# Attention with all PSUM banks until the first layer begins, weight decoding moved, first batch's layer output kept in DRAM, branch at the end

## The chip, the cores and the metric

The kernel runs on one core of a Trainium2 chip. The metric is device microseconds of one execution. One profiled execution gives the trace; its rows are in us from the start of its span.

## The reference, cut to what matters

```
scores = q @ k.T / sqrt(64);  scores = cap * tanh(scores / cap)      # 4 batches, 12 heads, 448 tokens, head size 64, fp32
attn = exp(scores - max) / (sum + 1e-9);  x = attn @ v               # heads joined: x is 1792 x 768
h = max(x @ w1, x @ w2, x @ w3)                                      # layer 1, w 768 x 768
y = h @ moe_w_out                                                    # layer 2, 768 x 768
u = sigmoid(y @ w_gate) * (y @ w_val)                                # layer 3, 768 x 1536 each
out = u @ moe2_w_out                                                 # layer 4, 1536 x 768
```

q, k and v are float32, all seven weight matrices float64.

## The kernel before

**Numbers.** Weights arrive as pairs of 32-bit words. `widths` (L44) loads a block of 128x768 of them (768 KB, tile `wraw`) and decodes it into float32 (`wf`): one operation on ACT (L51), four on DVE (L52 to L55). `parts` (L58) splits `wf` into a rounded high part `wh` (ACT, L61) and the remainder `wl` (POOL, L62). `product` (L76) makes one 128x448 block of a layer for one batch: 18 matmuls, six each of high by high, high by low and low by high. `wraw`, `wf`, `wh` and `wl` have two buffers each, so weights run about two blocks ahead. `col_block` (L65) loads one such block; layer 1 needs 18 (six column blocks j of three matrices). For batch 0 they are decoded, and stored decoded in DRAM (`ws`); later batches load them from there.

**Attention.** Heads are taken in pairs: 24 pairs, six a batch. `prepare` (L108) turns a pair's k and q with TensorE into a PSUM tile `tr` and splits them into kh, kl, qh, ql. `Pair.scores` (L171) forms score groups 0, 1, 2 (896 columns, two PSUM banks) and a half group; ACT applies tanh (L190), which frees the PSUM, and exp (L198). Sums over the keys are formed by POOL (L201, group 0 + 1) and DVE (L203, L206). `weigh` (L208) multiplies by v, `finish` (L220) normalises on DVE and splits x (ACT L235, POOL L236). `sc` and `tr` share two buffers of two banks, `pv` has two banks, and the layer products the remaining two (`mm`).

**Order.** Iteration n of the loop at L427 emits: loads of pair n+2, scores of pair n, `weigh` and `finish` of pair n-1, `prepare(n+1)`; from n = 7 it also takes three steps of `first_layers` (L419), a step being one `product` of layer 1 for batches 0, 1 and 2. Batch 3's x goes to DRAM (`xs`, L238) and is read back after the attention (L457 to L462) for its layer 1, with all eight PSUM banks. Then layer 2 (six weight blocks, four batches), layer 3 (12 blocks j, each of gate and value weights for four batches) and layer 4. Layer 4 decodes the 12 blocks of `wo2` one by one (L354) while it accumulates its first four output tiles, and then does ten more tiles from the kept weights.

**Queues.** All loads and stores are issued on SP's queue, in order. The build moves instructions ahead of program order where buffers allow, so some matmuls of layer 1 stand between those of the attention; each engine then runs its list in order.

**Branch.** The whole computation stands twice: for a small cap (`compute(False)`, the path that runs) and for any cap (`compute(True)`). A flag made from cap is read by every engine at the start (L483), before the If.

## Time and profile before

| | |
|---|---|
| median of three runs (lowest, highest) | 1165.6 us (1165.25, 1174.87) |
| profiled execution: its time, its span | 1164.32 us, 1162.5 us |
| busy share PE, PEld, DVE, ACT, POOL | 96%, 80%, 44%, 39%, 28% |
| matmuls | 5640 |
| HBM read, written | 86.31 MB, 13.96 MB |

```
PE   5889889999999999999999999999999999899998
DVE  3765987734242424117333333333333336763331
ACT  3667557566665553333222111111111124443331
POOL 1323545454544444554110111111111112510000
```

Each digit is the busy share, in tenths, of one fortieth of the span (29 us). A busy PE is not a PE at its peak, since queued matmuls overlap: how many matmuls a stretch holds says more than its busy time.

### The profile page before, as it was taken

The page shows a single profiled execution, that of the slowest core. Times are in us where ns is not written, and L with a number is a line of the kernel's source. Part 1 is how long each engine was busy: PE and PEld are TensorE (multiplying, and loading weights), DVE is VectorE, ACT ScalarE, POOL GpSimd, SP SyncE. Part 2 cuts the span into 40 slices and gives each one's busy share as a digit, 9 for nine tenths or more (in the row PEclk, how much of TensorE's full clock was granted, in tenths as well). Part 3 has the DMA queues.
Part 4 walks back from the last instruction along what each step waited for, and adds up shares of the span by engine and source line. Part 5 has one row for each costly group of instructions (what it writes and reads, how often), then busy time and mean ns, then how long its engine had stood idle before and what let it go on. Part 6 is the DMA issues. An engine that isn't in the chain of part 4 may idle for free.

```text
span 1162.5 us, 14670 instructions
## 1 busy us (share of the span) xinstructions
PE 1110.2 (96%) x5640; PEld 932.2 (80%) x5640; DVE 508.1 (44%) x804; ACT 456.8 (39%) x754; POOL 328.0 (28%) x193
## 2 busy tenths in 40 slices
PE   5889889999999999999999999999999999899998
PEld 2335666677767677899999999999999999899997
DVE  3765987734242424117333333333333336763331
ACT  3667557566665553333222111111111124443331
POOL 1323545454544444554110111111111112510000
PEclk9999899999999999999999999999999999899999
DMA  4643465633333323333111111111111111420011
GB/s 102 184 130 91 127 179 167 206 103 101 93 101 102 86 84 103 114 109 119 55 55 55 55 55 55 55 55 55 55 55 55 55 55 55 162 68 31 28 36 36
DMA packets 123359, 101.32 MB, mean 87 GB/s; under 512 B 70544, under 2 KB 112528, under 8 KB 123280
## 3 DMA queue, kind: packets, MB, share of 16 engines
q1 hardware_dynamic: 123280, 100.29, 29.1%
q8 instruction: 46, 0.75, 0.3%
q14 instruction: 33, 0.27, 0.1%
HBM read 86.31 MB, written 13.96 MB: 86 GB/s over the span
## 4 chain that ended last, share of the span: by engine, by line
PE 55%; issue 2%; POOL 1%; DVE 1%; ACT 1%; DMA 0%; POOLq 0%
PE mm L80 43%; PE mm L323 12%; POOL w L359 1%; DVE wf L55 0%; DVE wf L54 0%; DMA xr<-xs 0%; ACT w L358 0%; ACT wf L51 0%; POOL w2last L359 0%; DVE us L318 0%; ACT x L461 0%; DVE o L338 0%; ACT us L317 0%; DVE wf L53 0%; DVE wf L52 0%
## 5 line engine op out<-in xcount | busy, mean ns | idle before, releaser
L62 POOL TENSOR_TENSOR wl<-wf,wh 128x768 fp32r<-128x768 f32 x102 | 193.4, 1897 | 481.0 <-PE mm L80 389.8
L80 PE MATMUL mm<-y,wh 128*128 128x448 f32 x1152 | 249.1, 365 | 0.0
L80 PEld LDWEIGHTS mm<-y,wh 128*128 128x128 f32 x1152 | 216.3, 188 | 17.1
L80 PE MATMUL mm<-x,wh 128*128 128x448 f32 x864 | 198.5, 375 | 5.5 <-ACT x L461 2.2
L80 PEld LDWEIGHTS mm<-x,wh 128*128 128x128 f32 x864 | 160.5, 190 | 36.4 <-issue 9.5
L61 ACT CAST wh<-wf 128x768 fp32r<-128x768 f32 x102 | 84.9, 832 | 158.0 <-PE mm L80 121.0
L323 PE MATMUL mm<-w,us 128*128 128x384 f32 x756 | 136.1, 339 | 5.8 <-POOL w L359 5.8
L323 PEld LDWEIGHTS mm<-w,us 128*128 128x128 f32 x756 | 133.8, 191 | 6.5 <-POOL w L359 6.4
L80 PE MATMUL mm<-y,wl 128*128 128x448 f32 x576 | 132.3, 365 | 0.0
L80 PEld LDWEIGHTS mm<-y,wl 128*128 128x128 f32 x576 | 108.2, 188 | 8.6
L80 PE MATMUL mm<-x,wl 128*128 128x448 f32 x432 | 100.1, 366 | 0.0
L292 DVE TENSOR_TENSOR u<-mm,sg 128x448 f32<-128x448 f32 x48 | 29.8, 621 | 158.8 <-PE mm L80 158.8
L190 ACT ACTIVATE e<-sc,tsc 128x896 f32<-128x896 f32 x96 | 84.4, 910 | 33.3 <-PE sc L185 33.1
L289 ACT ACTIVATE sg<-mm 128x448 f32<-128x448 f32 x48 | 26.2, 546 | 166.0 <-PE mm L80 166.0
L198 ACT ACTIVATE e<-e,capb 128x896 f32<-128x896 f32 x96 | 88.1, 951 | 0.9
L52 DVE TENSOR_SCALAR wf<-wf 128x768 f32<-128x768 f32 x60 | 41.4, 694 | 105.5 <-ACT wf L51 105.4
L80 PEld LDWEIGHTS mm<-x,wl 128*128 128x128 f32 x432 | 81.3, 188 | 6.9
L318 DVE TENSOR_TENSOR us<-u,us 128x128 fp32r<-128x128 f32 (+1 forms) x192 | 54.8, 304 | 71.9 <-ACT us L317 71.9
L51 ACT ACTIVATE wf<-wraw 128x768 f32<-128x768 f32 x60 | 54.6, 911 | 75.7 <-POOL wl L62 57.4
L54 DVE SCALAR_TENSOR_TENSOR wf<-wraw,wf 128x768 int32<-128x768 int32 x60 | 82.1, 1372 | 1.5
L203 DVE TENSOR_TENSOR sum<-sum,e 128x896 f32<-128x896 f32 x24 | 32.3, 1347 | 107.4 <-ACT e L198 91.2
L317 ACT CAST us<-u 128x128 fp32r<-128x128 f32 (+1 forms) x192 | 48.5, 284 | 77.0 <-PE mm L323 73.8
(83 smaller groups left out, 1200.9 us busy)
## 6 DMA issues: line engine op xcount, KB each, us to landing
wf<-ws SPq DMA_DIRECT2D x54, 384.0 KB, 3.1
wraw<-in_moe_w_dram SPq DMA_DIRECT2D x18, 768.0 KB, 4.7
wraw<-in_moe_w_out_dram SPq DMA_DIRECT2D x18, 768.0 KB, 4.3
wraw<-in_moe_w_gate_dram SPq DMA_DIRECT2D x12, 768.0 KB, 4.3
wraw<-in_moe_w_val_dram SPq DMA_DIRECT2D x12, 768.0 KB, 4.4
ws<-wf SPq DMA_DIRECT2D x18, 384.0 KB, 2.7
kn<-in_k_dram SPq DMA_DIRECT2D x24, 192.0 KB, 3.3
qn<-in_q_dram SPq DMA_DIRECT2D x24, 192.0 KB, 3.6
```

The source lines that it names most:

```text
L51: nc.scalar.activation(wf, high.bitcast(F32), AF.Abs)
L52: nc.vector.tensor_scalar(wf, wf, LEAST, MOST, ALU.max, ALU.min)
L54: nc.vector.scalar_tensor_tensor(wi, high, -0x40000000, wi, ALU.bitwise_and, ALU.bitwise_or)
L61: nc.scalar.copy(wh, wf)
L62: nc.gpsimd.tensor_sub(wl, wf, f(wh))
L80: nc.tensor.matmul(ps, a[:, c, :], x[:, m, c, :], start=(n == 0), stop=(n == len(passes) - 1))
L190: nc.scalar.activation(e, sc[:, :w, :S], AF.Tanh, scale=tsc)
L198: nc.scalar.activation(e, e, AF.Exp, scale=1.0 if self.general else capb)
L203: nc.vector.tensor_add(self.sum, self.sum, e)
L317: nc.scalar.copy(us[:, 0, t, d], s)
L318: nc.vector.tensor_sub(us[:, 1, t, d], s, f(us[:, 0, t, d]))
L323: nc.tensor.matmul(pss[hf][:, :HALF], us[:, a, t, :], w2[fc][ww][:, hf * HALF : (hf + 1) * HALF], start=(fc == 0 and m == 0), stop=(fc == ...
```

## The change

- The attention before layer 1 (n up to 6) has a PSUM pool of its own with three two-bank buffers for `sc` and `tr`; at n = 7 it is closed, and `mm` and the old pool of two buffers take its banks. Until n = 6, `prepare(n+1)` is emitted before `weigh` of pair n-1.
- After iterations 1 to 6, the first six weight blocks of layer 1 are decoded and stored in `ws`; batch 0 loads these and decodes the other twelve.
- For batch 0 of layer 1, the remainders `wl` and of h are formed on DVE; for pairs 4 to 12 the group sum and the remainder of x too (`adds`).
- Batch 3's x stays in SBUF, its layer 1 is part of the interleaved steps, and h of batch 0 (2.75 MB) goes to DRAM at n = 18 and comes back in six parts during the last steps. Layer 2 takes the batches in the order 1, 2, 3, 0. After the attention, six new banks and the two of `mm` are taken in turn.
- `wo2` is decoded in layer 3, a block per j, and stored in DRAM (`ws2`); layer 4 loads the decoded blocks.
- Loads of the first pair's q go on ACT's queue; the tail of q has a zero-filled tile of 128 rows; the first pair's kh and qh are copied by ACT.
- `compute(False)` always runs; the flag is read at n = 4 and the If around `compute(True)` stands at the end.

```diff
+    EARLY = 6
-    xs = dram.tile([KC, P, S], F32, name="xs")
+    hs = dram.tile([P, 2 * KC * S], F32, name="hs")
+    ws2 = dram.tile([NF, P, DM], F32, name="ws2")
...
-        nc.gpsimd.tensor_sub(wl, wf, f(wh))
+        (sub or nc.gpsimd.tensor_sub)(wl, wf, f(wh))
...
+        other = nc.scalar if n == 0 else nc.sync
-        nc.sync.dma_start(out=qn, in_=main(q))
+        other.dma_start(out=qn, in_=main(q))
...
-        copy = nc.vector.tensor_copy if n < NP else nc.scalar.copy
+        copy = nc.vector.tensor_copy if 0 < n < NP else nc.scalar.copy
...
+            self.adds = nc.vector if NP - 2 <= n <= 2 * NP else nc.gpsimd
...
-                nc.gpsimd.tensor_add(self.sum, self.e[0], self.e[1])
+                self.adds.tensor_add(self.sum, self.e[0], self.e[1])
...
-            if x is not None:
-                nc.scalar.copy(x[:, 0, p, :], xn)
-                nc.gpsimd.tensor_sub(x[:, 1, p, :], xn, f(x[:, 0, p, :]))
-            else:
-                nc.sync.dma_start(out=xs[p], in_=xn)
+            nc.scalar.copy(x[:, 0, p, :], xn)
+            self.adds.tensor_sub(x[:, 1, p, :], xn, f(x[:, 0, p, :]))
...
+                sub = None if kept else nc.vector.tensor_sub
-                wt, this = None, wt or col_block(wpool, w, j, ws[wi, j], kept)
+                wt, this = None, wt or col_block(wpool, w, j, ws[wi, j], kept or 3 * j + wi < EARLY, sub)
...
-                nc.gpsimd.tensor_sub(hb[i][:, 1, j, :], hm[i], f(hb[i][:, 0, j, :]))
+                (nc.gpsimd if kept else nc.vector).tensor_sub(hb[i][:, 1, j, :], hm[i], f(hb[i][:, 0, j, :]))
...
             wtv = col_block(wpool, wv, j)
+            nc.sync.dma_start(out=ws2[j], in_=widths(wpool, wo2[j * P : (j + 1) * P, :], [P, DM]))
...
-            wf = widths(wpool, wo2[fc * P : (fc + 1) * P, :], [P, DM])
+            wf = wpool.tile([P, DM], F32, tag="wf", name="wf", bufs=2)
+            nc.sync.dma_start(out=wf, in_=ws2[fc])
...
+            pp = es0.enter_context(tc.tile_pool(name="pp0", bufs=3, space=PSUM))
...
+                if n == 4 and once:
+                    once()
+                if n == NP + 1:
+                    es0.close()
+                    mm = first.enter_context(tc.tile_pool(name="mm", bufs=2, space=PSUM))
+                    pp = es.enter_context(tc.tile_pool(name="pp", bufs=2, space=PSUM))
+                    pools[3], pools[4] = pp, mm
+                    steps = first_layers(mm)
...
+                        if b == 3:
+                            nc.sync.dma_start(out=hs, in_=flat(hb[0]))
...
+                if n < NP:
+                    prepared = prepare(n + 1, loaded.pop(n + 1), pools)
                 if before is not None:
                     before.weigh()
                     before.finish()
-                if n + 1 < B * NP:
+                if NP <= n < B * NP - 1:
                     prepared = prepare(n + 1, loaded.pop(n + 1), pools)
+                if 0 < n <= EARLY:
+                    j, wi = divmod(n - 1, 3)
+                    wf = widths(wpool, (w1, w2, w3)[wi][:, j * P : (j + 1) * P].rearrange("(c p) f -> p c f", p=P), [P, KC, P])
+                    nc.sync.dma_start(out=ws[wi, j], in_=wf)
...
+        hb[0] = new_act2("h")
+        for i, _ in enumerate(steps):
+            if i < KC:
+                part = slice(i * 2 * S, (i + 1) * 2 * S)
+                nc.sync.dma_start(out=flat(hb[0])[:, part], in_=hs[:, part])
+        mm = Banks((*[six] * 6, mm, mm))
...
-    with tc.If(flag > 0) as branch:
-        compute(False)
-    with branch.Else():
-        compute(True)
+    compute(False, read_flag)
+    with tc.If(flags[0] < 1):
+        compute(True, None)
```

## Rows read from the trace of the kernel before

**Rows 1.** Stages: length, busy us (instructions) of PE, PEld, DVE, ACT, POOL; clock; DMA.
```profile
9.38:99.78 90.40, 75.95 (x346) 35.37 (x347) 54.18 (x84) 53.98 (x67) 23.88 (x14) 0.96 0.51 136
99.78:227.79 128.01, 113.70 (x562) 78.38 (x561) 103.88 (x118) 79.95 (x110) 65.17 (x34) 0.93 0.55 161
227.79:422.42 194.63, 194.63 (x1033) 142.56 (x1032) 72.38 (x113) 116.94 (x158) 94.87 (x57) 1.00 0.37 99
476.00:971.95 495.95, 495.95 (x2449) 459.57 (x2448) 169.28 (x228) 115.67 (x178) 94.18 (x53) 1.00 0.20 63
971.95:1027.71 55.76, 49.48 (x266) 48.22 (x265) 46.98 (x87) 26.29 (x73) 26.65 (x11) 0.94 0.34 114
1027.71:1156.80 129.09, 129.08 (x743) 128.76 (x743) 40.93 (x144) 40.20 (x138) 0.00 (x0) 1.00 0.13 41
```

**Rows 2.** The same view for TensorE's matmuls of line 80 alone.
```profile
99.78:227.79 128.01, 59.57 (x268) 0.93 0.55 161
```

**Rows 3.** Timeline of the start: start, duration, engine, line, idle time before.
```profile
0.74 0.40 SPq L476 DMA_DIRECT2D capb<-in_cap_dram  x1
3.51 0.15 DVE L482 TENSOR_SCALAR bounded<-sq 128x1 int32<-128x1 f32 x1
4.33 0.78 SPq L98 DMA_DIRECT2D kn<-in_k_dram  x1
...
10.80 0.69 DVE L123 CAST kh<-tr 128x512 fp32r<-128x512 f32 x1 [6.03 <-PE tr L120]
...
12.80 0.74 PE L185 MATMUL sc<-qh,kh 64*128 64x448 f32 x2 [2.04 <-DVE qh L127]
...
20.80 0.27 PE L117 MATMUL tr<-ident,kt 128*128 128x128 f32 x1
```

**Rows 4.** Stages again: two iterations of the attention before layer 1.
```profile
61.90:73.58 11.68, 10.31 (x50) 4.29 (x49) 10.46 (x17) 9.03 (x12) 2.34 (x2) 1.00 0.27 61
...
88.96:99.78 10.82, 10.14 (x51) 4.28 (x50) 5.61 (x9) 7.24 (x10) 1.42 (x2) 1.00 0.29 65
```

**Rows 5.** DVE's and POOL's timeline in layer 3: a decode with and without POOL beside it.
```profile
913.82 1.95 POOL L62 TENSOR_TENSOR wl<-wf,wh 128x768 fp32r<-128x768 f32 x1 [1.86 <-ACT wh L61]
...
914.10 2.48 DVE L54 SCALAR_TENSOR_TENSOR wf<-wraw,wf 128x768 int32<-128x768 int32 x1
...
917.91 0.55 DVE L52 TENSOR_SCALAR wf<-wf 128x768 f32<-128x768 f32 x1
...
919.08 0.96 DVE L54 SCALAR_TENSOR_TENSOR wf<-wraw,wf 128x768 int32<-128x768 int32 x1
```

**Rows 6.** DVE's timeline, the group sum; groups by line, a remainder taken by DVE.
```profile
64.43 1.09 DVE L203 TENSOR_TENSOR sum<-sum,e 128x896 f32<-128x896 f32 x1 [0.28 <-POOL sum L201]
...
L279 DVE TENSOR_TENSOR y<-mm,y 128x448 fp32r<-128x448 f32 x24 | 14.8, 622 | 39.4 <-ACT y L278 39.4
```

**Rows 7.** SP's and TensorE's timeline: a decoded weight block from load to use.
```profile
409.61 11.27 SPq L69 DMA_DIRECT2D wf<-ws  x3
...
423.15 2.70 PE L80 MATMUL mm<-x,wh 128*128 128x448 f32 x12
```

**Rows 8.** DMA issues, from the page: KB each, median us to landing.
```profile
wf<-ws SPq DMA_DIRECT2D x54, 384.0 KB, 3.1
```

**Rows 9.** TensorE's timeline where attention ends, and in layer 4.
```profile
464.82 1.46 PE L80 MATMUL mm<-x,wh 128*128 128x448 f32 x6 [0.76 <-issue]
...
471.25 1.94 PE L80 MATMUL mm<-x,wh 128*128 128x448 f32 x7 [1.77 <-ACT x L461]
...
993.05 27.98 PE L323 MATMUL mm<-w,us 128*128 128x384 f32 x144 [4.04 <-POOL w L359]
1022.78 4.26 PE L323 MATMUL mm<-w,us 128*128 128x384 f32 x23 [1.75 <-POOL w L359]
```

**Rows 10.** ACT's and POOL's timeline in layer 3, weights of a new block.
```profile
908.76 0.84 ACT L61 CAST wh<-wf 128x768 fp32r<-128x768 f32 x1 [5.54 <-PE mm L80]
...
910.11 1.85 POOL L62 TENSOR_TENSOR wl<-wf,wh 128x768 fp32r<-128x768 f32 x1 [23.52 <-PE mm L80]
```

More of the change, by code (lines that the diff above doesn't have):

```diff
@@ L56, in widths, with parts @@
         return wf
-    def parts(wpool, wf, shape):
+    def parts(wpool, wf, shape, sub=None):
         wh = wpool.tile(shape, F32R, tag="wh", name="wh")
@@ L73, in col_block @@
                 nc.sync.dma_start(out=keep, in_=wf)
-        return parts(wpool, wf, shape)
+        return parts(wpool, wf, shape, sub)
     def product(ps, w, x):
@@ L96, in rest @@
             return src[b, h0 : h0 + 2, NT * P :, :]
+        other = nc.scalar if n == 0 else nc.sync
         nc.sync.dma_start(out=kn, in_=main(k))
-        nc.sync.dma_start(out=qn, in_=main(q))
-        nc.sync.dma_start(out=qt, in_=rest(q).rearrange("h p d -> p h d"))
+        other.dma_start(out=qn, in_=main(q))
+        other.dma_start(out=qt[:TAIL], in_=rest(q).rearrange("h p d -> p h d"))
         for e in range(2):
@@ L162, in less_max, with __init__, tile @@
                 nc.vector.tensor_sub(e, e, top[rows, :S])
+    class Banks:
+        def __init__(self, pools):
+            self.pools, self.n = pools, 0
+        def tile(self, shape, dt, **kw):
+            self.n += 1
+            return self.pools[self.n % len(self.pools)].tile(shape, dt, **kw)
     class Pair:
@@ L274, in layer2 @@
             wt = col_block(wpool, wo, j)
-            for i, h in enumerate(hb):
+            for i in (1, 2, 3, 0):
+                h = hb[i]
                 ps = mm.tile([P, 512], F32, tag="mm", name="mm")
@@ L378, in compute @@
     @with_exitstack
-    def compute(own: ExitStack, general):
+    def compute(own: ExitStack, general, once):
         act = own.enter_context(tc.tile_pool(name="act", bufs=4))
@@ L385, in new_act, with flat @@
             return act.tile([P, 2, KC, S], F32R, tag="act", name=name)
+        def flat(t):
+            return f(t).rearrange("p a c s -> p (a c s)")
+        first, es0 = own.enter_context(ExitStack()), ExitStack()
         with ExitStack() as es:
@@ L400, in compute @@
                     kts.append(kt)
+                    qt = const.tile([P, 2, D], F32, name=f"qt{i}")
+                    nc.gpsimd.memset(qt, 0.0)
+                    qts.append(qt)
                 vs = const.tile([P, NT, 2, D], F32, name=f"vs{i}")
@@ L417, in compute, with first_layers @@
             xb, hb = [], []
-            def first_layers():
+            def first_layers(mm):
                 wt = None
-                for b in range(3):
+                for b in range(B):
                     hb.append(new_act("h"))
-                    wt = yield from layer1(xb[b : b + 1], hb[b:], mm, wpool, sm, b > 0, wt, b < 2)
-            steps = first_layers()
+                    wt = yield from layer1(xb[b : b + 1], hb[b:], mm, wpool, sm, b > 0, wt, b < B - 1)
             before = None
@@ L428, in compute @@
                 b, p = n // NP, n % NP
+                if n == 4 and once:
[6 more added lines that the diff above has]
+                    steps = first_layers(mm)
                 if n < B * NP:
-                    if p == 0 and b < 3:
+                    if p == 0:
+                        if b == 3:
+                            nc.sync.dma_start(out=hs, in_=flat(hb[0]))
                         xb.append(new_act("x"))
@@ L433, in compute @@
                         loaded[n + 2] = load_pair(n + 2, pools)
-                    pair = Pair(n, prepared, pools, xb[b] if b < 3 else None, general)
+                    pair = Pair(n, prepared, pools, xb[b], general)
                     pair.scores(GROUPS[:2])
@@ L448, in compute @@
                 before = pair
-            for _ in steps:
-                pass
-        mm = own.enter_context(tc.tile_pool(name="mm8", bufs=8, space=PSUM))
         act2 = own.enter_context(tc.tile_pool(name="act2", bufs=4))
@@ L455, in new_act2 @@
             return act2.tile(shape or [P, 2, KC, S], dt, tag="act2", name=name)
-        x = new_act2("x")
-        for c in range(KC):
-            xr = sm.tile([P, S], F32, tag="hm", name="xr")
-            nc.sync.dma_start(out=xr, in_=xs[c])
-            nc.scalar.copy(x[:, 0, c, :], xr)
-            nc.vector.tensor_sub(x[:, 1, c, :], xr, f(x[:, 0, c, :]))
-        hb.append(new_act2("h"))
-        for _ in layer1([x], hb[3:], mm, wpool, sm, True, None, False):
-            pass
-        yb = [new_act("y")] + [new_act2("y") for _ in range(3)]
+        six = own.enter_context(tc.tile_pool(name="six", bufs=6, space=PSUM))
+        hb[0] = new_act2("h")
[4 more added lines that the diff above has]
+        mm = Banks((*[six] * 6, mm, mm))
+        yb = [new_act2("y") for _ in range(3)] + [new_act("y")]
         layer2(hb, yb, mm, wpool)
@@ L482, in tile_kernel, with read_flag @@
     nc.vector.tensor_scalar(bounded, sq, CAP_MAX**2, None, ALU.is_le)
-    flag = nc.values_load(bounded[0:1, 0:1], min_val=0, max_val=1)
-    with tc.If(flag > 0) as branch:
-        compute(False)
-    with branch.Else():
-        compute(True)
+    def read_flag():
+        flags.append(nc.values_load(bounded[0:1, 0:1], min_val=0, max_val=1))
+    flags = []
+    compute(False, read_flag)
+    with tc.If(flags[0] < 1):
+        compute(True, None)
 _INS = ["q", "k", "v", "cap", "moe_w1", "moe_w2", "moe_w3", "moe_w_out", "moe2_w_gate", "moe2_w_val", "moe2_w_out"]
```

31 lines of the change are left out of this document (14 added, 17 removed).

## The prediction

> **What bounds the kernel now.** I read the stages first [rows 1], cut where `prepare` transposes kt of pairs 0, 7, 13 and 23, and where the last two layers change over. The question for each is how many matmuls it holds for its length. From pair 13 to 23 TensorE is busy in all 194.63 us: an iteration takes 19.46 us. In layers 1 to 3 after the attention it is busy throughout too, 495.95 us for 2448 products' matmuls, 0.2026 us each. So an iteration's 54 layer matmuls cost 10.94 us and its share of the attention 8.52. These are the floors for the rest.
>
> Two stretches lie far above them. Pairs 0 to 7 take 90.40 us, 12.9 a pair, although TensorE needs 8.5. The next six iterations, where batch 0's weights are decoded, take 128.01 us. They hold 268 layer matmuls [rows 2]: 268 x 0.2026 + 6 x 8.52 = 105.4, so 22.6 us are lost. DVE is busy in 103.88 of the 128.01 us (81%), against 72.38 of 194.63 later. Layer 4's first part is the third: 266 matmuls in 55.76 us, while the 743 after it take 0.1737 us each, 46.2 for 266. The 9.6 us lost are waits for `w2` of 4.04 and 1.75 us [rows 9], a smaller one, and the granted clock, 0.94 of full speed there (it is one of two levels, so about 3.3 us of lost half-clock time after the longest wait).
>
> Last I read the start: SP issues the first k load at 4.33 us, after the flag, and scores begin at 12.80 [rows 3].
>
> **The change part by part.** Durations are of the profiled execution, 1164.3 us, which is 1.3 below the median of 1165.6.
>
> *Start.* With no flag to wait for, k follows cap's load on SP at 1.14 (0.74 + 0.40) instead of 4.33: 3.2 us. kt's loads no longer stand behind two loads of q on SP (the k load's issue took 0.78), and kh and qh are copied by ACT while DVE subtracts, where DVE did four operations in the 2.0 us from 10.80 to 12.80 [rows 3]. Together I take 4.5 us, between 3 and 5; scores then begin at 8.3.
>
> *Pairs 0 to 6.* Today tanh must free the second score buffer before `prepare` and the next scores. With three buffers this wait goes and the fullest engine is late next, DVE. Without decoding it works 7.24 us an iteration in the steady stretch [rows 1]. One undisturbed decode is about 3.0 us (0.55 twice and 0.96 twice, L53 and L55 being of the forms of L52 and L54) [rows 5]. So n = 1 to 3 want 10.2 us each; n = 4 and 5 also the group sum (1.09) and x's remainder (0.62) [rows 6], 11.9; n = 6, whose kh and qh ACT copies, 10.6. That is 65.0 us. An iteration of today with two decodes had DVE busy 10.46 of 11.68 us, 90% [rows 4], and at that share it would be 72. I take 68, as the new buffer also removes some of the waits in that row. ACT is not the bound: 7.24 us in the iteration without a decode, about 8.2 with one [rows 4]. `prepare(1)` ends 8.0 us after the first scores today [rows 3]; with the transposes no longer behind the third group's tanh I take 5.7, so pair 1 stands at 14 and pair 7 at 82, against 99.78: 17.8 us earlier, 13.3 of them beyond the start's 4.5. Bounds: pair 7 at 79 by DVE's plain sum, at 93 if nothing becomes faster than today's 13.2 a pair.
>
> *Iterations 7 to 12.* The 20 layer matmuls that today ran before pair 7 (288 - 268) come into this stretch: floor 288 x 0.2026 + 6 x 8.52 = 109.5 us. On DVE: six times 7.24; 1.7 of `adds` each (10.2); 17 weight remainders of 768 columns, 0.93 each by columns from the sum's 1.09 for 896 (15.8); five of h at 0.62 (3.1); twelve decodes at 3.0 (36): 108.5 us. POOL is then idle, and this decides what a decode costs: L54 took 2.48 us beside a POOL subtraction and 0.96 without [rows 5]. Two engines that both want 109 us do not finish in 109; today's fuller one was at 81%, the two with no POOL beside them I put at 91%: 120 us, 8 less than today. Bounds 109.5 and 133 (108.5 at 81%). Pair 13 is then prepared at 202, 25.8 us early.
>
> *Iterations 13 to 23.* TensorE is the bound and no work is added to it; batch 3's x costs ACT and POOL what batch 2's does in the same row. New is the store of h of batch 0, 2.75 MB on SP's queue ahead of the weight loads. A load of 384 KB lands in 3.1 us [rows 8]; the DMA engines move 99 GB/s at a busy share of 0.37 [rows 1], so some 270 GB/s when full, and the store takes about 10 us. The weights loaded at 409.61 are multiplied at 423.15 [rows 7]; less 3.1 for landing and 0.84 for the copy [rows 10], 9.6 us are to spare. I take 1 us, between 0 and 10. The Trainium skill speaks against more optimism (DMA: Bandwidth & Descriptors, section Queues, rings and completion order): on one ring the descriptors are consumed in order, so a load queued behind the store waits for all of it. By that rule the term would be 0.5 us for the load behind it and about 2.5 for one with less to spare; no run shows so long a transfer yet.
>
> *End of the attention.* TensorE waits 0.76 and 1.77 us around the reading back of x [rows 9]; x of batch 3 now stays. I take 2.5 us off. The parts of h come back beside a load of 384 KB every 3.65 us: 843 KB, 3.1 us of full DMA, hidden with little to spare, and not wanted before layer 2.
>
> *Layer 3* gets twelve decodes: 36 us of DVE and 11 of ACT, where DVE is busy 169.28 and ACT 115.67 of 495.95 us. I cost it at nothing, since new weights are used well after they are made: the copy at 908.76 and the subtraction from 910.11 to 911.96 [rows 10] serve a product that starts 3.65 us (18 x 0.2026) after the copy could start. If that cover goes, see the third rival.
>
> *Layer 4* loses its decode and keeps a load, a copy (0.84) and a subtraction of 1.85 us a block, against 24 matmuls, 4.2 us. Of 9.6 us lost I take back 9; between 6 and 9.6.
>
> *Flag and branch.* Every engine reads the flag at n = 4, and a taken branch stands behind the last store. From the compare (3.51) to SP's next instruction (4.33) is 0.8 us today. I add 1 us; 0 to 4, as today's program also jumps at its end.
>
> **Sum:** 1164.3 - 4.5 - 13.3 - 8 + 1 - 2.5 - 9 + 1 = 1129.
>
> **The rivals.** *DVE is the bound of iterations 1 to 12.* It takes over POOL's subtractions and sums. If its share stays at 90% before pair 7 and 81% after, pair 7 comes 4 us later and the next stretch takes 133: 1129 + 4 + 13 = 1146. For: both rows of today show DVE the fullest engine but one. Against: part of its waiting was for POOL.
>
> *TensorE alone is the bound.* Then 65 and 109.5 us hold: 1129 - 3 - 10.5 = 1115, TensorE busy throughout from pair 7 on. For: DVE without POOL does the same in less. Against: both engines would have to be full at once.
>
> *Layer 3 begins to wait (slower).* The third decode of each block shares the two `wf` buffers, and its store holds one of them. If it falls between a block's last product and the next weights, the chain is 0.9 (ACT, about its copy's 0.84) + 3.0 (DVE) + 3.1 (store, by the load of the same size) = 7.0 us. It decides once more than about 2.7 us lands there (3.65 less the copy's 0.84). Then 4.3 us are lost eleven times, with about 3.3 us of clock each as after the 4.04 us wait: 1129 + 11 x 7.6 = 1213. Against: a block lasts 29 us (144 x 0.2026), and the decode may run anywhere in it.
>
> *The third buffer does nothing,* the decode iterations do not shorten, and only start, end of the attention and layer 4 pay: 1164.3 - 4.5 - 2.5 - 9 + 2 = 1150.
>
> **How the numbers follow.** Forecast 0.50, DVE 0.20, TensorE 0.18, third buffer 0.07, layer 3 0.05. The range takes in the two neighbours and the third-buffer case: 1110 to 1150, the bottom 5 us below the TensorE case for the start's and the branch's bounds. About 1% can be told from no change here, 1154 to 1177. All cases but layer 3's are centred below 1154, and the upper ends of the DVE and third-buffer cases reach it: faster 0.90, within 1% 0.05, slower 0.05.
>
> **What would show it.** Scores near 8.3 us; pair 7's kt at 82 and pair 13's at 202; later iterations still 19.46 us apart but for one after n = 18; no wait for x at the end of the attention; layer 3 at 144 matmuls in 29 us; layer 4's first 288 matmuls at 0.174 us. Pair spacings of 13 us before pair 7, or gaps in front of the weights in layer 3, would make it wrong.

## The result, and the profile after

The changed kernel takes 1127.56 us (median; 1126.46 to 1128.6) against 1165.42 for the kernel before in the same series: ratio 0.9666, 95% interval 0.9622 to 0.971. The forecast was 1129, in a range of 1110 to 1150. Its profiled execution took 1127.63 us with a span of 1125.8, against 1164.32 and 1162.5. HBM reads rose to 94.77 MB and writes to 20.05 MB, POOL fell to 22% of the span, and TensorE stayed at 96%. The kernel before took 1161.6 to 1167 us in most executions and 1171 to 1176 in the others, which moves the ratios from series to series, so the times of the changed kernels are set side by side below.

The stages of the changed kernel, cut where [rows 1] is cut (length, busy us and instructions of PE, PEld, DVE, ACT, POOL, clock, DMA share, GB/s): pair 0's kt to pair 7's, to pair 13's, to 14's, to 23's, to layer 4's first matmul, and layer 4 in two parts.

```profile
6.08:82.24 76.16, 60.41 (x325) 32.43 (x325) 57.04 (x86) 54.13 (x68) 13.89 (x8) 0.98 0.61 161
82.24:202.34 120.10, 110.46 (x585) 80.78 (x583) 98.74 (x148) 79.81 (x109) 0.00 (x0) 0.96 0.57 169
202.34:226.97 24.63, 21.66 (x105) 15.44 (x104) 14.13 (x21) 14.21 (x20) 7.64 (x4) 0.93 0.73 215
226.97:398.99 172.02, 172.02 (x929) 127.63 (x928) 63.64 (x101) 106.26 (x144) 87.43 (x53) 1.00 0.38 107
...
398.99:943.60 544.61, 544.61 (x2696) 498.70 (x2695) 213.41 (x290) 144.26 (x216) 119.95 (x68) 1.00 0.28 90
...
943.60:999.36 55.76, 55.76 (x323) 55.76 (x322) 32.19 (x67) 23.57 (x76) 20.59 (x11) 1.00 0.32 97
999.36:1118.55 119.19, 119.15 (x688) 118.83 (x686) 35.26 (x126) 35.82 (x125) 0.00 (x0) 1.00 0.10 32
```

Set beside the kernel before, cut at the same events (its iteration 13 is taken as a tenth of the 194.63 us of [rows 1]):

| stretch | before | after | gain | forecast |
|---|---|---|---|---|
| span's start to pair 7's kt | 99.78 | 82.24 | 17.5 | 17.8 |
| pairs 7 to 13 | 128.01 | 120.10 | 7.9 | 8 |
| pair 13 to 14 | 19.46 | 24.63 | -5.2 | 0 |
| pairs 14 to 23 | 175.17 | 172.02 | 3.1 | -1 |
| pair 23 to layer 4 | 549.53 | 544.61 | 4.9 | 2.5 |
| layer 4 to the last copy | 184.88 | 174.95 | 9.9 | 9 |
| after the last copy | 5.67 | 7.25 | -1.6 | -1 |
| sum | 1162.5 | 1125.8 | 36.7 | 35.3 |

The last two rows part at the start of the last copy. The sums agree, but misses of 2 to 5 us in both directions cancel: that the total is met to 1.4 us is in part luck. The twelfth decode, too, ends behind pair 13 (its third DVE operation stands at 207.66), so pairs 7 to 14 are the fairer stretch: 144.73 us, where 139.5 were forecast. The next views show where the time went.

**Start.** The first scores begin at 11.45 us, not at 8.3. The timeline of the changed kernel's start (start, duration, engine, line, idle time before, in brackets):

```profile
1.19 0.77 SPq L100 DMA_DIRECT2D kn<-in_k_dram  x1
1.35 0.21 POOL L421 MEMSET qt<- 128x128 f32 x1
...
2.00 1.30 SPq L104 DMA_DIRECT2D kt<-in_k_dram  x2
...
5.36 0.64 ACTq L102 DMA_DIRECT2D qt<-in_q_dram  x1
...
9.03 0.45 PE L122 MATMUL tr<-ident,qt 128*128 128x128 f32 x1 [1.89 <-DMA qt<-in_q_dram]
...
10.86 0.53 ACT L129 CAST qh<-tr 128x448 fp32r<-128x448 f32 x1 [0.76 <-DVE kl L127]
...
11.45 0.74 PE L199 MATMUL sc<-qh,kh 64*128 64x448 f32 x2 [1.97 <-ACT qh L129]
```

The k load went out early as foreseen (1.19). But the load of q's tail, on ACT's queue, was issued only at 5.36, although ACT had issued q's other load at 0.74. It writes a tile that POOL has just filled with zeros. The fill alone does not explain 5.36: kt's load writes a tile filled in the same way, and went out on SP's queue at 2.00, 0.9 us after that fill was over (0.87 + 0.21). On ACT's queue the load of q's tail went out just behind the landing of the first k load (1.19 + 4.1), and in a_pool_back too (5.27, k landed at 5.2); what ties it to that landing is not shown. TensorE waits 1.89 us for it at 9.03. And ACT's copy of qh waits for DVE's subtraction of kl (0.76), so the split of a pair does not run side by side on two engines: from TensorE's last transpose to the first scores it takes 1.97 us, 2.04 before [rows 3].

**The handover from pair 7 to 8, and the iterations behind it.** Stages again, the first two iterations of the 120.10 us:

```profile
82.24:104.17 21.93, 14.65 (x69) 9.85 (x68) 14.78 (x21) 14.70 (x20) 0.00 (x0) 0.77 0.65 194
104.17:123.27 19.10, 19.10 (x106) 14.19 (x105) 14.54 (x21) 13.39 (x18) 0.00 (x0) 1.00 0.50 140
```

The five iterations 8 to 12 take 98.17 us together, 19.10 to 20.61 each; in the longest one stands a single wait for tanh of 1.42 us. That is nearly TensorE alone. The loss is at the front. Iteration 7 holds one product (18 matmuls, 3.65 us) and its share of the attention (8.2 us), and takes 21.93. The timeline of what TensorE waits for there:

```profile
85.00 1.08 DVE L217 TENSOR_TENSOR sum<-sum,e 128x896 f32<-128x896 f32 x1
...
86.53 1.25 DVE L220 TENSOR_TENSOR sum<-sum,e 64x448 f32<-64x448 f32 x2
...
87.80 0.69 DVE L127 TENSOR_TENSOR kl<-tr,kh 128x512 fp32r<-128x512 f32 x1
88.41 0.55 DVE L54 TENSOR_SCALAR wf<-wf 128x768 f32<-128x768 f32 x1
...
89.47 0.62 DVE L131 TENSOR_TENSOR ql<-tr,qh 128x448 fp32r<-128x448 f32 x1
...
90.23 0.74 PE L199 MATMUL sc<-qh,kh 64*128 64x448 f32 x2 [7.28 <-DVE ql L131]
90.74 0.60 PE L199 MATMUL sc<-qh,kl 64*128 64x448 f32 x2
```

The kh of pair 7 was ready at 84.66 (ACT, 84.07 + 0.59), but its kl stands behind sums and x's remainder in DVE's list; qh waits for kl (it ends at 89.06), and ql also for part of a decode. In pair 6 the first scores start when qh is there (qh ends at 75.98, scores at 76.07, ql begins at 76.45), and so they do in pair 13. Here they start 0.15 us after the end of ql, and nothing else of TensorE's runs before. The reason is argued, not shown by a run: ql is the last to read `tr` of pair 7, which lies in the PSUM pool that is closed here, and `mm` and the new pool take its banks. The first work in the new pools starts 0.14 to 0.15 us after the end of that ql in all twelve kernels here that change pools; in k_step_first it is a layer product, which does not read ql. TensorE then runs at the lower clock: the granted clock is 0.54 of full speed from 90.23 to 97.00 and 1.00 from there to 104, and two matmuls of 448 columns take 0.60 us, where they take 0.36 later. The 7.28 us and about 3 us of lower clock (0.46 x 6.77, an estimate) make up the 10 us that this iteration takes over its 11.9.

**Iteration 13** takes 24.63 us, 5.5 over the next. TensorE's timeline:

```profile
209.67 0.47 PE L199 MATMUL sc<-ql,kh 64*128 64x448 f32 x2 [0.78 <-DVE ql L131]
...
211.70 0.47 PE L199 MATMUL sc<-qh,kh 64*128 64x448 f32 x2 [0.96 <-ACT e L204]
...
212.42 4.27 PE L82 MATMUL mm<-x,wh 128*128 128x448 f32 x12
```

DVE is busy nearly without a gap from 198 to 212, with the last two decodes, two weight remainders and a pair's sums and x; the waits add up (these two, 1.02 us for the copy of new weights at 204.07 and 0.17 at 208.22), and after them 12 matmuls take 4.27 us (0.36 each, against 0.20). The granted clock from 212 to 217 is 0.66 of full speed, a mix of its two levels.

**Iterations 14 to 23** are 19.11 us apart (19.46 before). The zero-filled tail of q makes its transpose one of 128 rows. TensorE's timeline, first of the changed kernel, then of the kernel before at the same place:

```profile
380.32 0.27 PE L122 MATMUL tr<-ident,qt 128*128 128x128 f32 x1
380.34 2.68 PE L82 MATMUL mm<-x,wh 128*128 128x448 f32 x12
```

```profile
403.43 0.27 PE L120 MATMUL tr<-ident,qt 64*128 64x64 f32 x1
403.63 1.08 PE L80 MATMUL mm<-x,wh 128*128 128x448 f32 x4
```

The product follows the 128-row transpose after 0.02 us, and followed the 64-row one after 0.20. Another 0.09 us lie ahead of that transpose: it starts 0.42 us behind the first of q's other three, and 0.33 when it has 128 rows. TensorE counts as busy in both; the step is seen in the starts alone.

**End of the attention, layer 4.** There is no wait on TensorE from 398.99 to 943.60; the three of before (0.76, 0.40 and 1.77 us; [rows 9] has two) are gone. Layer 4's first blocks run without a gap, 240 matmuls in 41.60 us, 0.1733 each:

```profile
951.95 37.60 PE L337 MATMUL mm<-w,us 128*128 128x384 f32 x216
989.39 4.32 PE L337 MATMUL mm<-w2last,us 128*128 128x384 f32 x24
```

### The profile page after: what moved, and what is told of

It is laid out like the page before. It is cut to its first block, busy times and chain, and to the rows that moved or that the text cites. A ratio compares the mean times of both kernels' runs of the same rounds, so it can differ in the third digit from the quotient of the medians.

```text
span 1125.8 us, 14706 instructions
## 1 busy us (share of the span) xinstructions
PE 1084.7 (96%) x5640; PEld 930.2 (83%) x5640; DVE 515.4 (46%) x838; ACT 458.1 (41%) x756; POOL 251.5 (22%) x159
## 3 DMA queue, kind: packets, MB, share of 16 engines
HBM read 94.77 MB, written 20.05 MB: 102 GB/s over the span
## 4 chain that ended last, share of the span: by engine, by line
PE 84%; DVE 8%; ACT 4%; issue 2%; DMA 1%; POOL 0%; SPq 0%; ACTq 0%; DVEq 0%
PE mm L82 58%; PE mm L337 16%; PE pv L230 4%; PE sc L199 3%; ACT e L204 2%; ACT e L212 1%; PE pv L232 1%; PE sc L196 1%; DVE sum L220 1%; DVE wf L56 1%; DVE sum L217 1%; DVE wf L57 1%; DVE kl L127 1%; ACT wf L53 1%; PE tr L118 1%
## 5 line engine op out<-in xcount | busy, mean ns | idle before, releaser
L64 POOL TENSOR_TENSOR wl<-wf,wh 128x768 fp32r<-128x768 f32 x84 | 157.1, 1871 | 554.3 <-PE mm L82 355.0
L82 PE MATMUL mm<-x,wh 128*128 128x448 f32 x864 | 193.5, 374 | 1.5 <-ACT wh L63 1.4
L337 PE MATMUL mm<-w,us 128*128 128x384 f32 x756 | 132.8, 334 | 0.0
L337 PEld LDWEIGHTS mm<-w,us 128*128 128x128 f32 x756 | 131.2, 188 | 0.0
L332 DVE TENSOR_TENSOR us<-u,us 128x128 fp32r<-128x128 f32 (+1 forms) x192 | 63.4, 355 | 89.4 <-ACT us L331 88.6
L204 ACT ACTIVATE e<-sc,tsc 128x896 f32<-128x896 f32 x96 | 84.1, 909 | 17.8 <-PE sc L199 17.8
L54 DVE TENSOR_SCALAR wf<-wf 128x768 f32<-128x768 f32 x60 | 33.1, 553 | 113.2 <-ACT wf L53 113.2
L56 DVE SCALAR_TENSOR_TENSOR wf<-wraw,wf 128x768 int32<-128x768 int32 x60 | 80.3, 1339 | 1.7
L275 DVE TENSOR_TENSOR hm<-mm,hm 128x448 f32<-128x448 f32 x48 | 29.9, 623 | 102.6 <-PE mm L82 102.6
L217 DVE TENSOR_TENSOR sum<-sum,e 128x896 f32<-128x896 f32 x24 | 28.3, 1180 | 94.2 <-ACT e L212 93.4
```

What stands on the lines that cost most here:

```text
L56: nc.vector.scalar_tensor_tensor(wi, high, -0x40000000, wi, ALU.bitwise_and, ALU.bitwise_or)
L64: (sub or nc.gpsimd.tensor_sub)(wl, wf, f(wh))
L82: nc.tensor.matmul(ps, a[:, c, :], x[:, m, c, :], start=(n == 0), stop=(n == len(passes) - 1))
L204: nc.scalar.activation(e, sc[:, :w, :S], AF.Tanh, scale=tsc)
L217: nc.vector.tensor_add(self.sum, self.sum, e)
L332: nc.vector.tensor_sub(us[:, 1, t, d], s, f(us[:, 0, t, d]))
```

## The experiments

Each kernel is the changed one but for the edit shown, except e_qtail_only, which is the kernel before with one part of the change. Ratios are to the kernel before, run beside each; its fastest run lay between 1161.6 and 1163.1 us in every series, so medians of different series can be set side by side to about 2 us. Part of a difference between two profiles lies at the very end: from the start of the last copy to the end of the span pass 5.65 to 8.05 us in the changed kernels, with no tie to their edits.

**a_pool_back: the subtractions and sums back on POOL**

```diff
-            self.adds = nc.vector if NP - 2 <= n <= 2 * NP else nc.gpsimd
+            self.adds = nc.gpsimd
-                sub = None if kept else nc.vector.tensor_sub
+                sub = None
-                (nc.gpsimd if kept else nc.vector).tensor_sub(hb[i][:, 1, j, :], hm[i], f(hb[i][:, 0, j, :]))
+                nc.gpsimd.tensor_sub(hb[i][:, 1, j, :], hm[i], f(hb[i][:, 0, j, :]))
```

> The changed kernel with POOL forming the remainders of batch 0's layer 1 and the group sums and x remainders of all pairs again. Exclusive-access theory: a decode beside a POOL subtraction costs DVE up to 2.5 us an operation instead of 0.96, so iterations 8 to 12 go back from 19.6 to about 21 to 23 us each and pair 13's kt moves from 202 to 210 or later; 1135 to 1145 us in all. Rival, DVE's count of work decides: five microseconds an iteration leave DVE, pair 13 comes at 195 to 200 and the time falls to 1120 to 1125 us.

Measured: 1137.0 us (1136.45 to 1138.27), ratio 0.9739 (0.9667 to 0.981), so 9.4 us slower than the whole change. The stage from pair 7 to 13, and pieces of the timeline:

```profile
83.76:218.89 135.13, 116.28 (x584) 83.86 (x583) 93.14 (x117) 82.28 (x112) 66.98 (x36) 0.92 0.57 171
```

```profile
134.67 0.91 ACT L53 ACTIVATE wf<-wraw 128x768 f32<-128x768 f32 x1 [0.95 <-POOL wl L64]
...
136.43 2.03 POOL L64 TENSOR_TENSOR wl<-wf,wh 128x768 fp32r<-128x768 f32 x1 [0.68 <-POOL x L249]
136.80 2.48 DVE L56 SCALAR_TENSOR_TENSOR wf<-wraw,wf 128x768 int32<-128x768 int32 x1
...
141.37 0.47 PE L199 MATMUL sc<-qh,kh 64*128 64x448 f32 x2 [2.10 <-ACT e L204]
...
189.94 2.90 POOL L215 TENSOR_TENSOR sum<-e 128x896 f32<-128x896 f32 x1 [2.06 <-ACT e L212]
190.80 2.46 DVE L54 TENSOR_SCALAR wf<-wf 128x768 f32<-128x768 f32 x1
192.81 2.14 POOL L64 TENSOR_TENSOR wl<-wf,wh 128x768 fp32r<-128x768 f32 x1
193.30 2.07 DVE L55 TENSOR_SCALAR wf<-wf 128x768 int32<-128x768 int32 x1
```

The stretch takes 135.13 us, 15.0 more than in the changed kernel; iteration 13 behind it takes 19.11 instead of 24.63, so the two together take 9.5 more. The signs of the first theory came out (pair 13 at 218.89, 1137.0 us). DVE has less to do here, 93.14 of 135.13 (69%) against 98.74 of 120.10 (82%), but its operations get longer: 16 of 116 take at least 0.25 us more than the median of their shape and line, 16.5 us more in all, and every one of the sixteen stands beside a POOL operation. L54 and L55, 0.56 us otherwise, take up to 2.46 and 2.08. In the changed kernel POOL is idle in this stretch, and not one is longer. Ten of the sixteen, with 11.6 us of the 16.5, lie on the chain of work that ended last.

There is a second price, the buffers: POOL's remainder takes 1.8 to 2.6 us where DVE's takes 0.95, queues behind POOL's other work, and frees the `wf` buffer late; ACT's first decode step waits for that (0.95 above), DVE for ACT (20.5 us in eight waits, against 4.0 in five in the changed kernel), and TensorE for a tanh that stands behind on ACT (2.10 above). No run separates the two. The Trainium skill (SBUF — State Buffer, section SBUF: two separate sides) has DVE and GpSimd contend for one port pair, with the loser blocked for the whole instruction. The trace agrees in that DVE is lengthened beside POOL alone; 25 other operations of DVE overlap one of POOL's and are not longer.

**b_two_buffers: two score buffers before layer 1 instead of three**

```diff
-            pp = es0.enter_context(tc.tile_pool(name="pp0", bufs=3, space=PSUM))
+            pp = es0.enter_context(tc.tile_pool(name="pp0", bufs=2, space=PSUM))
```

> The changed kernel with two score buffers before layer 1 instead of three. Forecast's theory: tanh must free a buffer before prepare again, pairs 1 to 7 go back towards 13 us each, pair 7's kt from 82 to 90 or more; 1135 us or more. Rival, DVE's work sets the pairs and the buffer nothing: pair 7 within 2 us of 82, time within 2 us of 1127.6.

Measured: 1135.49 us (1134.58 to 1137.39), ratio 0.9721 (0.965 to 0.9792). Pair 7 comes at 92.30, 10.1 us later, with pairs 9.3 to 14.2 apart. TensorE again waits for tanh at the score groups:

```profile
66.30 0.47 PE L199 MATMUL sc<-qh,kh 64*128 64x448 f32 x2 [0.50 <-ACT e L204]
```

DVE is less full than with three buffers, 62.10 of 86.22 us (72%) against 57.04 of 76.16 (75%). There are six such waits up to pair 7, 3.0 us together, as in the kernel before, and none in the changed one. They are the sign of the missing buffer but not the 10 us: most of these lie in matmuls that TensorE counts as busy (68.25 us for the 325 that took 60.41), and why is not shown. The third buffer is worth 8 to 10 us by the edit itself, and the rival that it does nothing falls.

**c_decode_layer4: `wo2` decoded in layer 4 again**

```diff
-            nc.sync.dma_start(out=ws2[j], in_=widths(wpool, wo2[j * P : (j + 1) * P, :], [P, DM]))
...
-            wf = wpool.tile([P, DM], F32, tag="wf", name="wf", bufs=2)
-            nc.sync.dma_start(out=wf, in_=ws2[fc])
+            wf = widths(wpool, wo2[fc * P : (fc + 1) * P, :], [P, DM])
```

> The changed kernel with the last matrix decoded in layer 4 as before. Theory: the 9.6 us of waits and half clock come back in layer 4 and layer 3 does not become shorter: 1136 to 1138 us. Rival, the decode in layer 3 costs layer 3 something that is given back: under 1134 us.

Measured: 1136.62 us (1135.75 to 1137.35), ratio 0.9734 (0.9663 to 0.9805), 9.1 us slower. The last copy moves from 1118.55 to 1128.53, 10.0 later (the 5.78 us behind it are 1.5 fewer), and the waits of [rows 9], 4.04 and 1.75 us, are back as 4.06 and 1.75:

```profile
964.78 10.19 PE L335 MATMUL mm<-w,us 128*128 128x384 f32 x48 [4.06 <-POOL w L371]
```

The stretch 429.13 to 935.00, layers 2 and 3 without the decodes, holds 2496 matmuls, where the changed kernel holds 2498: layer 3's decodes cost TensorE nothing, and the slower rival falls.

**d_branch_first: the If back at the start, around the computation**

```diff
-    flags = []
-    compute(False, read_flag)
-    with tc.If(flags[0] < 1):
+    flag = nc.values_load(bounded[0:1, 0:1], min_val=0, max_val=1)
+    with tc.If(flag > 0) as branch:
+        compute(False, None)
+    with branch.Else():
```

> The changed kernel with the flag read and the If and Else at the start, as before. Theory: the first k load moves from 1.19 to 4.3 us and the first scores from 11.4 to about 14.6, while the end loses the taken branch: span after the last copy 5.7 instead of 7.3 us; together 1 to 2 us more, 1129 us. Rival, q's tail on ACT's queue sets the start and the branch nothing: first scores within 1 us of 11.4, time 1126 us.

Measured: 1128.66 us (1127.79 to 1131.36), ratio 0.9669 (0.9597 to 0.9741). The scores begin 3.7 us later and pair 7's kt comes at 87.84, 5.6 later:

```profile
15.19 0.74 PE L199 MATMUL sc<-qh,kh 64*128 64x448 f32 x2 [1.96 <-ACT qh L129]
```

But pair 14 stands at 228.95, only 2.0 later: iteration 7 takes 19.27 us instead of 21.93, and iteration 13 23.15 instead of 24.63. From the start of the last copy 6.9 us pass instead of 7.3, where the theory wanted 5.7 for 7.3. That the branch at the end makes this part long is not borne out: a_pool_back and c_decode_layer4 have it there and take 5.65 and 5.78. By the medians 1.1 us of the 3.7 reach the end, and the runs of the two kernels overlap.

**e_qtail_only: the kernel before, with q's tail in a zero-filled tile of 128 rows**

```diff
-        qt = ld.tile([TAIL, 2, D], F32, tag="qt", name="qt")
+        kt, qt = kts[n % 2], qts[n % 2]
-        nc.tensor.transpose(qps[:, NT * P : S], qt.rearrange("p h d -> p (h d)"), ident[:TAIL, :TAIL])
+        nc.tensor.transpose(qps[:, NT * P : SK], qt.rearrange("p h d -> p (h d)"), ident)
...
+                    qt = const.tile([P, 2, D], F32, name=f"qt{i}")
+                    nc.gpsimd.memset(qt, 0.0)
+                    qts.append(qt)
```

> The kernel before with one part of the change alone: q's tail in a zero-filled tile of 128 rows, so that all eight transposes of prepare have the same shape. Theory, the step between 64-row and 128-row work makes TensorE wait: iterations 13 to 23 fall from 19.46 to 19.11 us, as in the changed kernel, and the time by 4 to 7 us to about 1159. Rival, the 0.35 us an iteration came from another part (x of batch 3 kept in SBUF, the new pools): 19.46 us stay, 1164 to 1165.

Measured: 1164.04 us (1162.57 to 1176.06), ratio 0.9998 (0.9954 to 1.0043). The iterations after pair 13 are 19.11 us apart, as in the changed kernel, so the 0.35 us is this part's. Yet the time stays, since the first scores move from 12.80 to 16.13:

```profile
10.14 0.61 SPq L99 DMA_DIRECT2D qt<-in_q_dram  x1
...
13.64 0.45 PE L119 MATMUL tr<-ident,qt 128*128 128x128 f32 x1 [3.65 <-DMA qt<-in_q_dram]
```

The load was issued at 5.85 before and comes at 10.14 now, behind the loads of the second pair. The part gains 3.5 us over the ten iterations from pair 13 to 23. Of the 3.3 us lost at the start 1.2 are left at pair 13 (229.00 against 227.79), and from pair 23 to the last copy it is 1.6 us slower; together that nearly takes the gain up.

**g_qtail_sp: q's tail of the first pair on SP's queue**

```diff
-        other.dma_start(out=qt[:TAIL], in_=rest(q).rearrange("h p d -> p h d"))
+        nc.sync.dma_start(out=qt[:TAIL], in_=rest(q).rearrange("h p d -> p h d"))
```

> The changed kernel with the tail of the first pair's q issued on SP's queue, only the main part on ACT's. Theory: the first scores waited for that tail, issued at 5.4 us on ACT's queue behind the first load's landing; they move from 11.4 to about 9 us. If the handover at pair 7 is not limited by something of its own, the time falls by 2 us to 1125.5. Rival, from the run with the branch first: of 3.7 us at the start only 2.0 were left after pair 13, so less than 1 us remains of it, 1127.

Measured: 1125.52 us (1123.76 to 1129.67), ratio 0.9661 (0.9599 to 0.9724). The start got worse, not better: SP issues the load at 6.98, behind others, and TensorE waits 3.27 us.

```profile
10.46 0.45 PE L122 MATMUL tr<-ident,qt 128*128 128x128 f32 x1 [3.27 <-DMA qt<-in_q_dram]
```

The scores begin at 12.87, and still pair 14 comes at 222.43 instead of 226.97. Iteration 7 takes 18.70 us and iteration 13 23.10. On SP the load stands behind those of the second pair's k and q and of v, so the run does not say what held it back on ACT's queue. The start's microseconds are not the end's; the gain of 2.0 us by the medians is not clear of this kernel's own spread of 5.9 us.

**h_handover and i_all: DVE relieved before pair 7, the first block loaded an iteration earlier** (i_all adds the edit of g_qtail_sp)

```diff
-            self.adds = nc.vector if NP - 2 <= n <= 2 * NP else nc.gpsimd
+            self.adds = nc.vector if NP < n <= 2 * NP else nc.gpsimd
...
+                if n == NP:
+                    ready = col_block(wpool, w1, 0, ws[0, 0], True)
```

> The changed kernel with two changes at the handover to layer 1: group sums and x remainders go to DVE for pairs 7 to 12 instead of 4 to 12, and the first weight block of layer 1 is loaded and split in iteration 6, on POOL. Theory: pair 7 waits 7.3 us for ql, behind sums and remainders in DVE's queue, and the first layer matmuls for a load issued at 87 us; the 21.9 us from pair 7 to 8 shrink by 4 to 8, and the time to 1120 to 1124. Rival: POOL's sums beside the early decodes cost DVE as much as they free (as in the run with POOL's work back), pair 7 comes 2 us later and the time stays within 2 us of 1127.6.

> The changed kernel with both: q's tail on SP's queue and the handover's two changes. If the two gains add, 1118 to 1122 us; if the handover sets its own pace, the same as the handover's changes alone.

Measured: 1130.28 us (1129.87 to 1130.43), ratio 0.9691 (0.9632 to 0.975), and 1129.51 (1128.98 to 1132.19), ratio 0.9682 (0.9624 to 0.9741). Neither gains: every run of both is slower than the changed kernel's slowest (1128.6). In h_handover the wait stays:

```profile
83.67 2.09 POOL L215 TENSOR_TENSOR sum<-e 128x896 f32<-128x896 f32 x1 [1.79 <-ACT e L212]
...
86.98 2.02 DVE L220 TENSOR_TENSOR sum<-sum,e 64x448 f32<-64x448 f32 x2
...
91.46 0.74 PE L199 MATMUL sc<-qh,kh 64*128 64x448 f32 x2 [7.65 <-DVE ql L131]
```

POOL's sum takes 2.09 us where DVE's took 1.05, and DVE's last sums take 2.02 us, 1.25 in the changed kernel, beside POOL's remainder of x: what leaves DVE comes back in part as longer operations, which is the rival's reason. Pair 7's kt comes at 83.11, 0.87 us later, and ql ends 8.2 us behind it instead of 7.8. In i_all the wait is 4.94 us, but iteration 13 takes 26.01.

**f_no_early: no block decoded early**

```diff
-    EARLY = 6
+    EARLY = 0
```

> The changed kernel without early decodes: all 18 blocks of batch 0 are decoded in iterations 7 to 12. Theory, DVE has time to spare before pair 7 only if its 3 us a decode are hidden there: pairs 1 to 6 fall to about 8 to 9 us, pair 7 comes 8 to 12 us earlier, and iterations 7 to 12 become DVE's, 21 us or more each, so that pair 13 comes 2 to 8 us later than 202; 1130 to 1136 us. Rival, the early decodes only move DVE's work from one stretch to another: pair 13 within 2 us of 202, 1127.

Measured: 1124.96 us (1124.73 to 1125.73), ratio 0.9635 (0.9569 to 0.97): 2.6 us *faster* than the change. But the edit does not do what was expected of it, since the build moves decodes ahead of program order here too. L56, the third of a decode's four DVE operations, up to pair 7, first in the changed kernel, then here, and this kernel's stage from pair 7 to 13:

```profile
0.00:82.24 82.24, 6.63 (x5) 0.98 0.60 158
```

```profile
0.00:82.02 82.02, 4.75 (x4) 0.98 0.56 144
...
82.02:204.38 122.36, 111.64 (x584) 80.01 (x583) 101.71 (x151) 80.77 (x110) 0.00 (x0) 0.97 0.55 160
```

Four decodes still stand before pair 7, where the changed kernel has five, thirteen instead of twelve lie in the next six iterations, and one in iteration 13 in both. So neither the theory nor its rival was put to the test, and pair 7 at 82.02 (82.24) says little. Iteration 13 takes 21.10 us, but iteration 12 23.82: together 44.92, against 19.63 + 24.63 = 44.27 in the changed kernel, so the loss there has moved and not shrunk. At the last copy this profile is 1.5 us ahead; the rest lies behind it.

**j_tail_rows: only the rows that q's tail leaves empty are filled**

```diff
-                    nc.gpsimd.memset(qt, 0.0)
+                    nc.gpsimd.memset(qt[TAIL:], 0.0)
```

> The changed kernel with only rows 64 to 127 of q's tail tile filled with zeros, so that the load of rows 0 to 63 waits for no fill. Theory: in all runs with the 128-row tile the first scores waited for this load (issued at 5.4 us here, at 10.1 in the kernel before with the tile alone); it is issued at 1.5 us now and the first scores come at 8.3 to 9 us instead of 11.4, pair 1 near 14; the time falls by 1.5 to 3 us. Rival: the handover at pair 7 or DVE takes it up and the time stays within 1 us of 1127.6.

Measured: 1122.9 us (1121.87 to 1125.53), ratio 0.9612 (0.9547 to 0.9678). This is the fastest kernel here; its slowest run is below the changed kernel's fastest (1126.46), though the two ratio intervals overlap. The load no longer writes what POOL fills and goes out at once:

```profile
1.49 0.69 ACTq L102 DMA_DIRECT2D qt<-in_q_dram  x1
...
9.84 0.74 PE L199 MATMUL sc<-qh,kh 64*128 64x448 f32 x2 [1.96 <-ACT qh L129]
```

In the changed kernel it went out 3.9 us later, though the fill of that tile was over at 1.56: how much of this is the fill and how much what the build then ordered ahead of the load is not separated. Pair 7's kt still comes at 82.33; the wait behind it is 4.93 instead of 7.28 us, so pair 13 is reached at 199.58, 2.8 us earlier. The profiled execution is this kernel's slowest, so the profile shows 2.1 of the 4.7 us.

**k_step_first: j_tail_rows, with layer 1's first step put ahead of pair 7's scores**

```diff
+                    if n == NP + 1:
+                        next(steps, None)
...
+                if n == NP:
+                    ready = col_block(wpool, w1, 0, ws[0, 0], True)
```

> The same with the first step of layer 1 ahead of pair 7's scores, its weight block loaded and split in iteration 6. Theory: TensorE's 7.3 us wait for ql of pair 7 is filled with the 3.65 us of that step and its clock stays higher, so pair 8 comes 3 to 6 us earlier than in the kernel with the tail rows alone and the time falls to 1119 to 1123 us. Rival: the step needs x of pair 5, which DVE makes late, and stands in front of the scores in TensorE's order; then the scores only come later and the time rises by 1 to 4 us.

Measured: 1125.08 us (1124.51 to 1126.47), ratio 0.9638 (0.9572 to 0.9703), no gain over j_tail_rows. The step too waits for ql:

```profile
86.56 0.62 DVE L131 TENSOR_TENSOR ql<-tr,qh 128x448 fp32r<-128x448 f32 x1
...
87.33 4.82 PE L82 MATMUL mm<-x,wh 128*128 128x448 f32 x12 [6.36 <-DVE ql L131]
```

Yet the product reads x, wh and wl, not ql; its weights were split by 83.3, and DVE makes the last of x only at 87.10 to 87.71, after the product has begun. So the rival's reason, late x, did not hold up its start. What it shares with ql is the PSUM pool that is closed there (ql reads `tr`), as argued above; no run here keeps that pool open.

**l_tail_no_early: j_tail_rows and f_no_early together**

```diff
-    EARLY = 6
+    EARLY = 0
-                    nc.gpsimd.memset(qt, 0.0)
+                    nc.gpsimd.memset(qt[TAIL:], 0.0)
```

> The changed kernel with the tail rows alone filled and without early decodes. If the two gains measured singly (4.7 us and 2.6 us) come from different stretches they add: 1120 to 1121 us. If both end in the wait for ql of pair 7, the time stays at 1122 to 1123 us.

Measured: 1123.85 us (1122.76 to 1124.39), ratio 0.9629 (0.9589 to 0.9669). The gains of 4.7 and 2.6 us do not add. Pair 7 comes at 80.25, about 2 us earlier than in either, but the wait for ql is 6.92 us as in f_no_early (4.93 in j_tail_rows), and iterations 12 and 13 take 45.02 us together, again four decodes standing before pair 7 and one in iteration 13.

## Why the prediction was right, and where it was not

*Start, mis-sized.* 4.5 us were forecast and 1.35 came (scores at 11.45, not 8.3). k's load went out 3.1 us earlier, as said. The step that failed is that nothing else would hold the scores up: q's tail did, and j_tail_rows, in which its load goes out at once, has them at 9.84. The other 1.3 us of the term do not show: the copies by ACT gain 0.07 (2.04 to 1.97), for ACT's qh waits for DVE's kl.

*Pairs 0 to 6, right by position.* Pair 7's kt came at 82.24, forecast 82, with 16.2 us gained behind the first scores where 13.3 were expected. That it was DVE that was late is shown by halves only: it is busy 11.75 of the 11.83 us of iteration 55.80 to 67.63, but 55.72 of the 65.29 from pair 1 to 7 (85%), TensorE 53.39. Five decodes lie before pair 7, not six; the sixth is the one in front of ql at the handover. No run took decodes away (f_no_early moved one), so what sets pair 7 to 82 is not settled. b_two_buffers shows the buffer's part.

*Iterations 7 to 12, right in sum, made otherwise.* 120 us were forecast and 120.10 came, with part of the last decode left for iteration 13, so the match is luck in part. The reason "POOL beside a decode" was right: in the kernel before 25 of DVE's 117 operations of this stretch are longer than the median of their shape, by 27.2 us in all, each beside POOL, and in the changed kernel none is. The 120 was argued as two engines that both want 109 us. DVE's instructions there do add up to 107.3 us by their durations (over its groups by line), beside the 108.5 of the forecast, but DVE is busy for 98.74: neighbours overlap in the trace, and so a sum of durations overstates an engine by 9%. TensorE's floor is nearly reached, as in the rival "TensorE alone", in five of six iterations (98.17 us, by 54 x 0.2026 + 8.2 = 19.1 each 95.7). The sixth, the handover, takes 10 us more than its 11.9 and makes the total: the change of PSUM pools was put at nothing, and behind it TensorE waits 7.28 us for ql and runs at the lower clock. That POOL's work belongs on DVE was right (9.4 us); how much of it is the lengthening and how much the chain of buffers is not separated.

*Iteration 13, not foreseen:* 5.2 us lost to DVE's backlog and the lower clock after four short waits, with the last decode in it. In a_pool_back and in the kernel before no decode lies in iteration 13, and it takes 19.11 and 19.40 us; there iteration 12 takes 24.81 and 24.26.

*Iterations 14 to 23.* 19.46 us each were forecast, 19.11 came: the 128-row tail was costed at nothing and is worth 0.35 us an iteration, by e_qtail_only. The store of h was put at 1 us and cost none. It was issued at 224.13, at the end of iteration 13 after that iteration's waits, although it stands at n = 18 in the program: the build moved it forward. It did what was feared on the queue. DMA issues from 220 to 242 us (KB each, median us to landing):

```profile
hs<-h SPq DMA_DIRECT2D x1, 2688.0 KB, 10.8
...
kn<-in_k_dram SPq DMA_DIRECT2D x1, 192.0 KB, 8.8
```

The store took 10.8 us, about the 10 worked out, and the k load behind it 8.8 us, where the median of all is 3.3. By the Trainium skill (DMA: Bandwidth & Descriptors, Queues, rings and completion order) the load is consumed behind the store, and the trace agrees: it landed at 236.0, the store at 234.9. But TensorE shows no wait from 226.97 on, so the slack of the loads covered it.

*End of the attention.* 2.5 us were forecast, 4.9 came: 2.93 are the three waits of before that are gone. Another 1.5 are the same waits where TensorE counts as busy: from 462.68 to 473.03 the kernel before runs 29 matmuls in 10.35 us, which at 0.2026 each take 5.88, so 4.47 us are lost there and not 2.93. These 4.47 are the whole difference in the 54 us behind pair 23.

*Layer 3, right:* 2446 matmuls in the 495.50 us to 943.60, 0.2026 each, no gap. *Layer 4, right:* 9.9 for 9, by c_decode_layer4 9.1 in all and 10.0 up to the last copy. *Flag and branch:* the profile has 1.6 us more behind the last copy, within 0 to 4, but with the same branch other kernels have the 5.7 of before, so no cost of the branch is shown; moving it back to the start costs 1.1 us in all, inside the spread of the runs.

The parts undone one by one give 9.4 (POOL's work), 7.9 (buffer), 9.1 (layer 4) and 1.1 (branch), 27.5 of 37.9. The stages show two more, 4.5 at the end of the attention and 3.1 from pair 14 to 23. What early decoding is worth is not known: EARLY = 0 moved one decode across pair 7, and its kernel is 2.6 us faster.

What stays open: the handover's wait for ql is 4.93 to 7.65 us in all runs; moving sums, weights or a step did not remove it, and a kernel that does not close the PSUM pool at this point was not run. Iterations 12 and 13 together take 42.7 to 45.6 us in all twelve kernels with the change of pools, against 2 x 19.11 later, and no kernel here removes that.

## What to carry to other kernels

Price a stretch by the floor of each engine, and take an engine's busy time, not the sum of its instructions' durations, before saying that two engines cannot both be full. Look at the length of single operations, too, and at all lines of a helper: in a_pool_back L56 of the decode looks undisturbed by its median (0.96 us), while L54 and L55 take up to four times as long beside POOL as without. At the change from one regime to the next (here when layer matmuls begin) look for the one instruction that the first work of the new regime waits for, and ask whether it needs that result or only the memory: the sum of the stages hides it. Check in the trace that an edit moved what it was to move, since the build orders the instructions anew. Filling only the part of a tile that no load will write let the load go out at 1.49 us instead of 5.36 here; another load into a filled tile went out 0.9 us behind its fill, so look at the order of the queue before blaming the fill.

## What the runs showed of the hardware

- A 64-row transpose between 128-row matmuls costs TensorE about 0.35 us a pair more than a padded one of 128 rows (19.46 against 19.11 us), though it is counted busy throughout.
- Operations of DVE take longer beside POOL's: 16 of 116 by 16.5 us in a_pool_back and 25 of 117 by 27.2 us in the kernel before, in the stretch from pair 7 to 13, each overlapping one of POOL's; none in the changed kernel, where POOL is idle there.
- After 7.28 us without work TensorE ran at the lower of its levels (granted clock 0.54 over the next 6.77 us; 0.60 us for two matmuls of 448 columns, later 0.36); in iteration 13 it did so after waits of 1.02, 0.17, 0.78 and 0.96 us within 8 us.
- A start that is 3.7 us later cost 1.1 us at the end by the medians, one 1.4 us later none (g_qtail_sp), both inside the spread of the runs: the later stages took the difference up.
